# Two-block chunks at the start, earlier W1, and engine orders written out, in a fused windowed-attention and feed-forward kernel

## The chip, the cores and the metric

The kernel runs on one core of a Trainium2 chip. A core has a matrix engine (TensorE, PE in the profile, with its weight loads shown as PEld), a vector engine (VectorE, DVE), an activation engine (ScalarE, ACT), a general engine (GpSimd, POOL) and SyncE (SP), which here only issues transfers. They run side by side, each through its own instructions in order, and wait for each other by semaphores. Transfers that POOL issues go through a software queue, and they change f32 to f16 on the way; those that SP issues go through a hardware queue.

The metric is the time of one execution on the device, in microseconds (us). The kernel before takes 310.35 us, the median of three runs (307.21 to 311.88).

## The reference

Inputs are q, k and v with 8 batches, 8 heads, 576 positions and a head size of 64, a gain vector of 512, and two weight matrices W1 (512 x 2048) and W2 (2048 x 512). All are f32.

```python
scores = (q @ k.T) / sqrt(64)
bias   = slope[h] * -abs(i - j)              # slope[h] = 2 ** -(h + 1)
mask   = (i - j >= 0) & (i - j < 128)
scores = where(mask, scores + bias, -1e9)
attn   = exp(scores - max(scores)); attn = attn / (sum(attn) + 1e-9)
x      = (attn @ v), heads side by side      # 8 x 576 x 512
xn     = (x - mean(x)) / sqrt(var(x) + 1e-6) * g
out    = x + maximum(xn @ W1, 0) @ W2
```

## The kernel before

**Blocks and chunks.** The 8 x 576 rows make 36 blocks of 128 rows. A row sees 128 keys back, so a block needs its own keys and those of the block before it; the first block of a pair of batches needs only its own. The list BLOCK puts the first two blocks of three of these pairs in front (places 0 to 5), then the rest. Blocks gather in chunks for the feed-forward part: CHUNKS has three chunks of 3, 3 and 2 blocks and seven of 4.

**Attention of block i** (function `attention`, L638). q and k are loaded, turned so that the head dimension lies on partitions (T tasks on TensorE with an evacuation ev or eT, or from block 9 on a transposing DMA, QT), and multiplied: S (L811). For the first five blocks a bias product Z (L827) puts distance and causality into the scores before S; from block 5 on the exp is multiplied by a table: mka and mkb (L866), one for each half of the heads. exa and exb are the exp on ACT (L859). pva and pvb (L887) multiply with v, which has a column of ones, so that the sum of a row comes with it; rc (L904) and nm (L908) divide. bn and ag take the statistics, mu and xs normalise (L947 for early chunks, L971 later), and x is turned by TX (L985) with an evacuation xt, or from block 6 on by a transposing DMA, XT.

**Loads.** Blocks 0 to 5 (SPANS = 0, 2, 4) come in pairs: `load_span` (L555) loads two blocks of q or k in f32 through SP, half of the heads at a time or all; casts cT (L706) on DVE, ACT or POOL make f16; T (L726) turns two f16 at a time as one f32. From block 6 (LOAD_CAST) q and k come through POOL's software queue as f16 (L573). v comes so from block 1 on. The weights, four parts of W1 (w0 to w3, L628) and four of W2 (w4 to w7, L630), come through the same queue.

**Feed-forward of chunk c** (function `mlp`, L1268). Chunks below SEVEN = 3 are plain: a task A{c}.{f} (L1285) multiplies one of 16 groups of W1's columns with the chunk's x, over four matmuls of up to 384 columns, into one PSUM bank; r{c}.{f} (L1300 on ACT, L1298 on DVE) is the relu; B{i}.{f} (L1319) multiplies with W2 and o adds x. Later chunks use seven products in place of eight, with sums made on DVE, for W2 (Pa to Pg, L1071), and from chunk BOTH = 8 on for W1 too (Ua to Ug, L1200). scaleW multiplies the gain into W1 before chunk SEVEN; earlier chunks multiply it into x.

**What sets the order.** Every step is a task with the engines that could do it, its costs and what it depends on. `Plan.run` (L131) plays the tasks through with a heap: on each engine it starts the ready task with the lowest due time, corrected by the tables PRI and HOLD; PICK says which engines a task may use, QUEUE in which order POOL's transfers go. What comes out is the order in which each engine's instructions are written. FILL (L274) puts products of a constant tile (`keep_warm`, L1366, matmuls at L1368) before named TensorE tasks; their result is never read. Masks may run on DVE or POOL by `e_m` (L863 to L866); PICK leaves them to the default, DVE.

```python
en = nc.vector if e == "DVE" else nc.gpsimd
en.tensor_tensor(out=pv, in0=pv, in1=mask[:, 2 * half : 2 * half + 2, :, lo:], op=ALU.mult)
```

Of the kernel before, what the change touches and what calls it, by code (L numbers as in the profile page):

```python
# [16 lines left out]
class Task:  # L17
    __slots__ = ("eng", "emit", "deps", "v", "lat", "acq", "rel", "left", "users", "ready", "end", "start", "name", "room", "chain")

    def __init__(self, name, eng, emit, deps, v, lat, acq, rel):  # L20
        self.name, self.eng, self.emit, self.v, self.lat = name, eng, emit, v, lat
        self.deps = [d for d in deps if d is not None]
        self.acq, self.rel = ([acq] if isinstance(acq, tuple) else acq or []), rel
        self.users, self.ready, self.end, self.start, self.room = [], 0.0, None, None, 0.0
        self.chain = []
# [29 lines left out]

class Plan:

    OVERLAP = {"ACT": 0.10, "DVE": 0.07, "POOL": 0.05}
    QUEUE_ROOM = {'DMA SP': 4.0, 'DMA ACT': 4.0, 'DMA POOL': 8.0}
    BEGIN = 0.75
    LANDING = {"DMA SP": (0.7, 1.3), "DMA ACT": (0.7, 1.3), "DMA POOL": (2.1, 1.4)}
    SHARES = {
        (True, 512): (0.66, 0.32), (True, 256): (0.66, 0.32), (True, 2048): (0.7, 0.4),
        (False, 512): (0.5, 0.5), (False, 256): (0.5, 0.5), (False, 2048): (0.5, 0.5),
    }
    LAST_OF_RUN = 1.0  # L70
    BEHIND = (2.5, 1.5)
    PRI: dict = {}
    HOLD: dict = {}
# [9 lines left out]
    def add(self, name, eng, emit, deps=(), v=0.0, lat=None, acq=None, rel=None):  # L83
        if not isinstance(eng, dict):
            eng = dict([eng])
        if lat is None:
            lat = 0.2 if "PE" in eng else 0.05 + max(self.OVERLAP.get(e, 0.0) for e in eng)
        eng = {e: c - self.OVERLAP.get(e, 0.0) for e, c in eng.items()}
        t = Task(name, eng, emit, deps, v + self.PRI.get(name, 0.0), lat, acq, rel)
        t.ready = self.HOLD.get(name, 0.0)  # L90
        self.tasks.append(t)
        return t

    def transfer(self, name, eng, issue, secs, room, emit, deps=(), v=0.0):

        queue = "DMA " + eng
        i = self.add(name + ".i", (eng, issue), emit, deps, v, lat=self.LANDING[queue][0])
        d = self.add(name, (queue, secs), None, [i], v, lat=self.LANDING[queue][1])
        i.room = d.room = room
        return i, d  # L100

    SLACK: tuple = (0, 0.4, 0)

    def slack(self, t, when):

        if "DMA POOL" in t.eng:
            return self.SLACK[2]
        return self.SLACK[0] if when < 30.0 else self.SLACK[1]

    def rates(self, queues):  # L110
        on = [q for q, x in queues.items() if x]
        if "DMA POOL" in on and len(on) > 1:
            others = [queues[q][0][0].name for q in on if q != "DMA POOL"]
            size = 512 if any(n[:2] in ("qs", "ks") for n in others) else 256 if any(n[0] in "qkv" for n in others) else 2048
            weight = queues["DMA POOL"][0][0].name[0] == "w"
            a, b = self.SHARES[weight, size]
            return {q: a if q == "DMA POOL" else b / (len(on) - 1) for q in on}
        return {q: 1.0 / len(on) for q in on}

    def skew(self, queue, now):  # L120

        if now >= 60.0:
            return 0.0
        early = 1.6 if self.early else 0.0
        if queue == "DMA POOL":
            return min(1.1, max(0.0, (now - 11.5) * 0.4)) + early
        if queue == "DMA SP" and now < 24.0:
            return (0.6 if self.mixed else 0.15) + early
        return 0.0

    def run(self):  # L131
        self.mixed = self.early = False
        again = []
        for r in self.rings:
            r.link()
        for t in self.tasks:
            t.left = len(t.deps) + len(t.chain)
            for d in t.deps + t.chain:
                d.users.append(t)
        engines = sorted({e for t in self.tasks for e in t.eng if not e.startswith("DMA")})  # L140
        queues = {e: [] for e in sorted({e for t in self.tasks for e in t.eng if e.startswith("DMA")})}
        free = dict.fromkeys(engines, self.BEGIN)
        avail = {e: [] for e in engines}
        state = {p: {b: self.opens.get((p, b), 0.0) for b in bs} for p, bs in self.banks.items()}
        held, waits, used = {}, {}, dict.fromkeys(queues, 0.0)
        for t in self.tasks:
            if t.rel is not None:
                waits[t.rel] = waits.get(t.rel, 0) + 1
        heap, n = [], 0
        for t in self.tasks:  # L150
            if t.left == 0:
                heap.append((max(self.BEGIN, t.ready), n, t))
                n += 1
        for x in self.opens.values():
            heap.append((x, n, None))
            n += 1
        heapq.heapify(heap)
        self.order, left, now = [], len(self.tasks), 0.0

        def done(t):  # L160
            nonlocal n
            for u in t.users:
                late = self.slack(t, t.end) if "PE" in u.eng and "PE" not in t.eng else 0.0
                u.ready = max(u.ready, t.end + (0.0 if t in u.chain else t.lat + late))
                u.left -= 1
                if u.left == 0:
                    heapq.heappush(heap, (u.ready, n, u))
                    n += 1

        def bank(t):  # L170
            got = []
            for p, key in t.acq:
                if key in held:
                    continue
                open_ = [(when, b) for b, when in state[p].items() if when is not None and when <= now + 1e-9]
                if not open_:
                    return False, None
                got.append((p, key, min(open_)[1]))
            return True, got

        while left:
            while heap and heap[0][0] <= now + 1e-9:
                t = heapq.heappop(heap)[2]
                if t is None:
                    continue
                for e in t.eng:
                    if e in queues:
                        if e == "DMA SP" and not queues[e] and queues["DMA POOL"] and t not in again:
                            again.append(t)
                            heapq.heappush(heap, (now + self.BEHIND[now >= 24.0], n, t))  # L190
                            n += 1
# [92 lines left out]
def kernel(  # L284
# [15 lines left out]
    P = 128  # L300
# [1109 lines left out]
```

## Time and profile before

| | |
|---|---|
| three timed runs | 307.21, 310.35, 311.88 us |
| span of the profiled execution, first to last instruction | 305.0 us |
| time around the span | not on the page; the timed runs are 2.2 to 6.8 us longer than the span |
| granted TensorE clock, mean | 1.000 |
| busy in 0 to 7 us: PE, DVE, ACT, POOL | 5.51 (60 filler matmuls), 2.01, 1.28, 1.38 of 7 |
| busy in 26.74 to 60 us: PE, DVE, ACT, POOL | 33.26, 28.64, 20.79, 22.54 of 33.26 |
| busy in 110 to 200 us: PE, DVE, ACT, POOL | 89.86, 75.19, 50.79, 38.38 of 90 |
| busy in 200 to 305 us: PE, DVE, ACT, POOL | 101.69, 87.19, 47.41, 0.00 of 105 |

The page's first part gives busy time of each engine over the span; the timeline lists instructions in order of time, neighbours of one kind merged, with the start, the time taken, the engine, the source line, and what is written and read (out<-in, buffer numbers left out); behind them in brackets the idle time before and what ended it. The waits view sums who waited for whom. TensorE's matmuls overlap, so a group's busy time is longer than the distance between starts times their number.

### The profile page before, as it was taken

To read this page: it belongs to the slowest core of one execution; us is meant where nothing else is said; L and a number is where in the kernel's file an instruction comes from. 1 tells how busy PE (TensorE), PEld (TensorE's weight loads), DVE (VectorE), ACT (ScalarE), POOL (GpSimd) and SP (SyncE) were. 2 spreads that over 40 slices of the span, in tenths; PEclk is the share of its full clock that TensorE was granted. 3 is DMA by queue.
4 is the path that set the end of the run, shared out by engine and by line. 5 is a ranking of instruction groups with operands and counts; after the bars stand their busy time and mean duration, and the time that the engine had idled before them with its cause. 6 is when DMAs were issued, how large, how long until landed. Compare 5 with 4: busy or idle time off the path is not lost.

```text
span 305.0 us, 7454 instructions
## 1 busy us (share of the span) xinstructions
PE 297.5 (98%) x2984; PEld 220.5 (72%) x2984; DVE 244.7 (80%) x597; ACT 164.8 (54%) x281; POOL 101.4 (33%) x132
## 2 busy tenths in 40 slices
PE   7989999999999999999999999999999999999995
PEld 7777756665774558765877577856777799999984
DVE  2778998677997479947983988999987889897883
ACT  1467943746776696436442956487733755235400
POOL 2993558735654337545405633100000000000000
PEclk9999999999999999999999999999999999999999
DMA  7999999999999999999999999961301500030043
GB/s 202 269 192 202 203 168 164 164 132 144 189 174 156 172 160 148 140 147 186 195 146 138 225 155 171 136 189 37 37 5 31 169 6 0 2 139 2 29 145 105
DMA packets 159652, 40.99 MB, mean 134 GB/s; under 512 B 145793, under 2 KB 155009, under 8 KB 159618
## 3 DMA queue, kind: packets, MB, share of 16 engines
q0 software_dynamic: 101680, 16.65, 76.9%
q1 hardware_dynamic: 57936, 23.87, 43.8%
q8 instruction: 23, 0.38, 0.5%
q14 instruction: 11, 0.09, 0.1%
q10 hardware_dynamic: 2, 0.00, 0.0%
HBM read 36.70 MB, written 9.44 MB: 151 GB/s over the span
## 4 chain that ended last, share of the span: by engine, by line
PE 86%; DMA 4%; DVE 4%; ACT 3%; issue 1%; SPq 0%; POOL 0%
PE fb L1285 30%; PE fb L1071 27%; PE u L1200 8%; PE fb L1319 7%; PE sc L811 5%; PE fb L887 5%; DMA qkt<-qk 3%; DMA qs<-in_q_dram 1%; ACT probs L859 1%; ACT ht L1300 1%; PE fb L726 1%; DVE st L927 1%; PE fb L1368 1%; DVE xb L908 1%; PE sc L827 1%
## 5 line engine op out<-in xcount | busy, mean ns | idle before, releaser
L1285 PE MATMUL fb<-xt,w1sb 128*128 128x512 f16 (+2 forms) x512 | 108.2, 353 | 0.6 <-DVE ot L1327 0.2
L859 ACT ACTIVATE probs<-sc 128x1024 f16<-128x1024 f32 (+1 forms) x72 | 67.9, 975 | 32.4 <-PE sc L811 30.9
L1300 ACT ACTIVATE ht<-fb 128x512 f16<-128x512 f32 (+2 forms) x109 | 58.3, 548 | 43.3 <-PE fb L1285 39.5
L1285 PEld LDWEIGHTS <-w1sb 128*128 128x128 f16 x512 | 55.2, 114 | 33.1 <-issue 1.3
L1071 PEld LDWEIGHTS <-ht 128*128 128x128 f16 x560 | 53.1, 98 | 9.9
L1071 PE MATMUL fb<-w2sb,ht 128*128 128x256 f16 x336 | 44.9, 273 | 0.0
L573 POOL DMA_DIRECT2D qk<-in_k_dram x34 | 28.7, 845 | 33.3 <-DMA qkt<-qk 23.5
L573 POOL DMA_DIRECT2D vx<-in_v_dram x36 | 30.7, 865 | 20.8 <-PE fb L887 8.2
L573 POOL DMA_DIRECT2D qk<-in_q_dram x34 | 28.8, 854 | 26.3 <-DMA qkt<-qk 12.8
L1071 PE MATMUL fb<-ks,ht 128*128 128x256 f16 x224 | 31.4, 273 | 0.0
L1319 PE MATMUL fb<-w2sb,ht 128*128 128x512 f16 x128 | 30.8, 379 | 0.2 <-ACT ht L1300 0.2
L866 DVE TENSOR_TENSOR probs<-probs,mreg 128x1024 f16<-128x1024 f16 (+1 forms) x46 | 30.1, 664 | 0.5 <-ACT probs L859 0.4
L887 PEld LDWEIGHTS <-probs 128*128 128x128 f16 x544 | 24.7, 97 | 7.5 <-ACT probs L859 0.6
L908 DVE SCALAR_TENSOR_TENSOR xb<-fb,rec 128x256 f16<-128x256 f32 x72 | 29.4, 416 | 0.8
L887 PE MATMUL fb<-vx,probs 128*128 128x65 f16 x496 | 27.2, 193 | 0.8 <-DVE xb L908 0.6
L904 DVE RECIPROCAL rec<-fb 128x4 f32<-128x4 f32 x72 | 12.2, 173 | 18.2 <-PE fb L887 18.0
L1083 DVE TENSOR_TENSOR ot<-fb,xb 128x512 f32<-128x512 f32 (+1 forms) x31 | 19.5, 634 | 7.2 <-PE fb L1071 6.7
L927 DVE BATCH_NORM_STATS2 st<-xb 128x6 f32<-128x512 f16 x36 | 24.4, 682 | 0.1
L811 PEld LDWEIGHTS <-qkt 64*128 64x128 f16 x496 | 14.9, 94 | 8.3 <-issue 7.4
L1223 DVE TENSOR_TENSOR ht<-u,probs 128x512 f16<-128x512 f32 x24 | 16.1, 686 | 5.3 <-PE u L1200 3.9
L1319 PEld LDWEIGHTS <-ht 128*128 128x128 f16 x128 | 11.4, 97 | 11.7 <-ACT ht L1300 0.4
L1213 ACT ACTIVATE probs<-u 128x512 f32<-128x512 f32 x21 | 12.2, 597 | 12.3 <-PE u L1200 12.2
(117 smaller groups left out, 397.0 us busy)
## 6 DMA issues: line engine op xcount, KB each, us to landing
out_dram<-ot SPq DMA_DIRECT2D x32, 256.0 KB, 3.6
vx<-in_v_dram POOLq DMA_DIRECT2D x28, 128.0 KB, 11.0
qk<-in_q_dram POOLq DMA_DIRECT2D x26, 128.0 KB, 11.2
qk<-in_k_dram POOLq DMA_DIRECT2D x26, 128.0 KB, 11.5
w1sb<-in_moe_w_ch_dram POOLq DMA_DIRECT2D x4, 512.0 KB, 10.6
w2sb<-in_moe_w_ch_dram POOLq DMA_DIRECT2D x4, 512.0 KB, 14.0
ks<-in_k_dram SPq DMA_DIRECT2D x4, 256.0 KB, 4.0
qs<-in_q_dram SPq DMA_DIRECT2D x4, 256.0 KB, 5.0
```

Source lines behind the costliest of these rows:

```text
L573: nc.gpsimd.dma_start(out=dst(p0, n), in_=src[b, :, s0 : s0 + n, :].rearrange("h p d -> p h d"))
L811: nc.tensor.matmul(scs[half][:, g, c0 : c0 + P], kt[rows, 1, hp, :], qkt[i][rows, 0, hp, :], start=not bias, stop=True, skip_group_check=True,
L859: nc.scalar.activation(out=o, in_=n_, func=AF.Exp, scale=inv_sqrt_d)
L866: en.tensor_tensor(out=pv, in0=pv, in1=mask[:, 2 * half : 2 * half + 2, :, lo:], op=ALU.mult)
L887: nc.tensor.matmul(pp[:, hh * (D + 1) : hh * (D + 1) + D + 1], probs[i][:, bank, slot, side * P : side * P + P], vx[i if side else before] ...
L908: nc.vector.scalar_tensor_tensor(out=xb[c][:, j, 256 * half : 256 * half + 256].rearrange("p (h d) -> p h d", d=D), in0=pp[:, :, 0:D], sca ...
L927: nc.vector.bn_stats(out=st[i][:, :], in_=xb[c][:, j, :])
L1071: nc.tensor.matmul(o, lhs(f, p), rhs(f), start=first and f == 0 and (p == 0 or key[0] != key[1]), stop=f == F2 - 1, skip_group_check=True)
L1200: nc.tensor.matmul(late[bank][:, FOURTH * f : FOURTH * f + FOURTH], w, rhs[kb], start=first and f == kb == 0, stop=kb == 1, skip_group_che ...
L1285: nc.tensor.matmul(fb[b][:, 0:n_], w1f[f // CB][:, kb, f % CB, :], xt[c][:, kb, 0:n_], start=(kb == 0), stop=(kb == NKB - 1),)
L1300: nc.scalar.activation(out=ht[c][:, f, 0:n_], in_=src, func=AF.Relu)
L1319: nc.tensor.matmul(pm[:, 0 : c1 - c0], ht[c][:, f, j * P : j * P + P], w2sb[f // CB][:, f % CB, c0:c1], start=(f == 0), stop=(f == NFB - 1),)
```

## The change

- CHUNKS begins with four chunks of two blocks in place of 3, 3 and 2. SEVEN and BOTH move by one, so that the same blocks are plain, and the same use seven products.
- In a two-block chunk, a task A{c}.{f} makes two groups of W1's columns, 256 columns each, into one bank, and one relu reads both. There are 8 such tasks for a chunk.
- Only blocks 0 and 1 are loaded as a span; q and k of blocks 2 to 5 come through POOL's queue as f16 and are turned one block at a time (T2 to T5). Only blocks 0 and 1 have their scores in two halves (SPLIT).
- The planner goes. ORDER is a text that names every task in the order of writing, with its engine (A for ACT, V for DVE, T for TensorE, G for POOL, S for SP) and, for TensorE, its PSUM bank; ~n stands for n filler matmuls. `Plan.run` reads it and asserts that what a task depends on stands before it. PRI, HOLD, PICK, QUEUE and FILL go. The engines of tasks are those that ORDER names: of the 62 masks, 44 stand on G and 18 on V. The fillers sum to 76, all before the 22nd TensorE task.
- On POOL, w0 stands behind the cast of the first half of k; w3, w1 and w2 follow behind q, k and v of blocks 2 and 3.

```diff
-QUEUE = ['cT0.00', 'cv0', 'v1', 'cT2.01', 'dist', 'dist1', 'v5', 'cT0.11', 'v2', 'dist1b', 'v3', 'w0', 'w3', 'w2', 'v4', 'w6', 'w1', 'dist1a', 'q6', 'k6', 'w4', 'w5', 'w7']
-FILL = {'T0.0': 60, 'G': 1, 'Gk': 1, 'Zb1': 9, 'T0.1': 4, 'Sb1': 13, 'Sa0': 1, 'pvb1': 10, 'pva0': 2, 'pvb0': 8, 'pva2': 10, 'Sa3': 1, 'pva3': 6}
...
+def Choice(names, full):
+    return dict(full)
...
     def run(self):
+
+        by, done, order, users = {}, set(), [], {}
+            by.setdefault(t.name, []).append(t)
+                users[t.rel] = users.get(t.rel, 0) + 1
+        owner, self.held = {}, {}
+
+        def ready(t):
+            if t.emit is None and id(t) not in done:
+                if all(ready(d) for d in t.deps):
+                    done.add(id(t))
+            return id(t) in done
+
+        for word in ORDER.split():
+            if word[0] == "~":
+                order.append((None, int(word[1:]), None))
+                continue
+            name, where = word.split(":")
+            t, e, b = by[name].pop(0), self.ENGINES[where[0]], int(where[1:]) if where[1:] else None
+            assert e in t.eng and all(ready(d) for d in t.deps), name
+            for n, (p, key) in enumerate(t.acq):
+                if key not in self.held:
+                    bank = b if n == 0 else self.banks[p][0]
+                    assert bank in self.banks[p] and owner.get((p, bank)) is None, name
+                    owner[p, bank], self.held[key] = key, (p, bank)
+            if t.rel is not None:
+                users[t.rel] -= 1
+                if users[t.rel] == 0:
+                    owner[self.held[t.rel]] = None
+            done.add(id(t))
+            order.append((t, e, self.held[t.acq[0][1]][1] if t.acq else None))
+        assert all(t.emit is None for ts in by.values() for t in ts)
+        return order
+
+
+ORDER = """
+iden1:G qs0.0.i:S iden2:G ks0.0.i:S dist:G sid0:V iden3:V dist00:G qs1.0.i:S sid6:V dist01:G sid5:V ks1.0.i:S sid3:V sid2:V sid7:V sid1:V sid4:V
+v0.i:S ~38 Za0:T0 cT0.00:A g.i:A cT0.10:G w0.i:G ~19 T0.0:T0 cT0.01:G eT0.00:V cT0.11:V q2.i:G ~7 Sa0:T0 eT0.01:V Zb0:T0 exa0:A T0.1:T1 k2.i:G Za1:T0
+eT0.10:V cv0:A v1.i:G eT0.11:A Sa1:T0 Sb0:T0 G:T2 q3.i:G exb0:A exa1:A k3.i:G Zb1:T0 Gc:V w3.i:G Sb1:T0 pvb0:T0 pva0:T1 exb1:A Gk:T2 v2.i:G rc1.0:V
+rc0.0:V nm0.0:V nm1.0:V v3.i:G ~8 T2:T1 mu0:V xs0:V Z2:T0 w1.i:G pva1:T0 ev2:V pvb1:T3 w2.i:G rc0.1:V Gkc:V S2:T0 rc1.1:V nm0.1:V k4.i:G TX0:T1
+nm1.1:V exa2:A T3:T2 bn0:V w4.i:G exb2:A mu1:V ev3:A xs1:V ~4 Z3:T0 w5.i:G bn1:V w6.i:G TX1:T0 S3:T0 xt1:A xt0:V q4.i:G exa3:A A0.14:T3 w7.i:G exb3:A
+A0.0:T2 r0.14:V pva3:T1 r0.0:A pva2:T0 A0.2:T3 rc0.3:V nm0.3:V rc0.2:V k6.i:G pvb3:T2 r0.2:V A0.12:T1 rc1.3:V nm0.2:V pvb2:T3 Z4:T0 nm1.3:V A0.6:T0
+rc1.2:V mu3:V xs3:V k5.i:G A0.4:T2 r0.6:A nm1.2:V r0.12:A mu2:V q5.i:G TX3:T3 xs2:V A0.8:T0 xt3:A ag0:V bn3:V TX2:T1 r0.8:A A0.10:T3 xt2:V r0.4:A
+ag3:V ag1:V bn2:V A1.6:T0 v4.i:G r0.10:V A1.4:T1 r1.6:A A1.12:T2 r1.4:A ln0:A A1.0:T3 q6.i:G rs0:A r1.12:A B0.0:T0 r1.0:V B1.0:T1 k7.i:G A1.2:T2
+B1.4:T1 q8.i:G B0.4:T0 T4:T3 B1.8:T1 ev4:V q7.i:G r1.2:V B0.8:T0 k8.i:G B1.12:T1 k8.i:G B0.12:T0 o1.0:V k9.i:G S4:T0 ag2:V sumT1.0:V A1.14:T3 q8.i:G
+exa4:A o0.0:V exb4:A T5:T2 q9.i:G sumT1.1:V r1.14:A A1.8:T1 ev5:V k10.i:G pva4:T0 pvb4:T3 S5:T0 mreg30:A rc1.4:V v5.i:G nm1.4:V mreg10:A T6:T2 exa5:A
+rc0.4:V nm0.4:V B3.0:T3 q11.i:G ev6:V mreg20:A B2.0:T0 mreg00:A r1.8:V q10.i:G exb5:A mu4:V A1.10:T2 xs4:V k11.i:G mreg01:A mreg11:A sumT0.0:V B3.4:T3
...
+"""
...
-    CHUNKS = [3, 3, 2, 4, 4, 4, 4, 4, 4, 4]
+    CHUNKS = [2, 2, 2, 2, 4, 4, 4, 4, 4, 4, 4]
-    WARM = 24.0
+    WARM = 14.0
-    SPLIT = 4
-    LOAD_CAST = 6
+    SPLIT = 2
+    LOAD_CAST = 2
-    BY_HALVES = [0, 2, 5]
+    BY_HALVES = [0]
-    SPANS = [0, 2, 4]
-    SLACK = (0, 1.0, 0)
-    SEVEN = 3
-    BOTH = 8
+    SPANS = [0]
+    SEVEN = 4
+    BOTH = 9
...
-            return {e: cost[e] for e in PICK.get((name, i), default).split()}
+            return Choice(default, cost)
...
+        two = 2 if nb == 2 else 1
         for at, f in enumerate(order):
+            if f % two:
+                continue
             key = f"A{c}.{f}"
             vm = v0 + at * per
 
             def e_a(e, b, f=f):
-                for kb in range(NKB):
-                    nc.tensor.matmul(
-                        fb[b][:, 0:n_], w1f[f // CB][:, kb, f % CB, :], xt[c][:, kb, 0:n_],
-                        start=(kb == 0), stop=(kb == NKB - 1),
-                    )
-            a = add(key, ("PE", 0.216 * nb), e_a, done + [scaled[f // CB] if fast else t_w[f // CB][1]], vm, acq=("fb", key))
+                for x in range(two):
+                    for kb in range(NKB):
+                        nc.tensor.matmul(
+                            fb[b][:, n_ * x : n_ * x + n_], w1f[f // CB][:, kb, (f + x) % CB, :], xt[c][:, kb, 0:n_],
+                            start=(kb == x == 0), stop=(kb == NKB - 1), skip_group_check=two > 1,
+                        )
+            a = add(key, ("PE", 0.216 * nb * two), e_a, done + [scaled[f // CB] if fast else t_w[f // CB][1]], vm, acq=("fb", key))
             xt.reads(c, a)
             plain_all[f // CB].append(a)
             if not fast:
                 plain[f // CB].append(a)
 
             def e_r(e, b, f=f, key=key):
-                src = fb[plan.held[key][1]][:, 0:n_]
+                src, o = fb[plan.held[key][1]][:, 0 : n_ * two], ht[c][:, f, 0:n_]
+                if two > 1:
+                    src, o = src.rearrange("p (f c) -> p f c", f=two), ht[c][:, f : f + two, 0:n_]
                 if e == "DVE":
-                    nc.vector.tensor_scalar(out=ht[c][:, f, 0:n_], in0=src, scalar1=0.0, scalar2=None, op0=ALU.max)
+                    nc.vector.tensor_scalar(out=o, in0=src, scalar1=0.0, scalar2=None, op0=ALU.max)
                 else:
-                    nc.scalar.activation(out=ht[c][:, f, 0:n_], in_=src, func=AF.Relu)
-            r_ = add(f"r{c}.{f}", {"ACT": 0.17 + 0.107 * nb, "DVE": 0.16 + 0.133 * nb}, e_r, [a], vm - 4.0, rel=key)
+                    nc.scalar.activation(out=o, in_=src, func=AF.Relu)
+            r_ = add(f"r{c}.{f}", Choice("ACT DVE", {"ACT": 0.17 + 0.107 * nb * two, "DVE": 0.16 + 0.133 * nb * two}), e_r, [a], vm - 4.0, rel=key)
             ht.writes(c, r_)
-            relu[f] = r_
+            for x in range(two):
+                relu[f + x] = r_
...
         for t, e, b in order:
-            if e == "PE":
-                keep_warm(FILL.get(t.name, 0))
+            if t is None:
+                keep_warm(e)
+                continue
```

More of the change, by code (lines that the diff above doesn't have):

```diff
@@ L1 @@
-import heapq
 from contextlib import ExitStack
@@ L94, in transfer @@
     def transfer(self, name, eng, issue, secs, room, emit, deps=(), v=0.0):
[L96 to L99, printed above, removed]
+        i = self.add(name + ".i", (eng, issue), emit, deps, v)
+        d = self.add(name, ("DMA " + eng, secs), None, [i], v)
         return i, d
[L102 to L118, printed above, removed]
@@ L160, in done @@
[L160 to L179, printed above, removed]
```

254 lines of the change are left out of this document (89 added, 165 removed).

## The prediction

> **What bounds the kernel now.** First the page: which engine is full, and where it is not.
>
> ```profile
> span 305.0 us, 7454 instructions
> PE 297.5 (98%) x2984; PEld 220.5 (72%) x2984; DVE 244.7 (80%) x597; ACT 164.8 (54%) x281; POOL 101.4 (33%) x132
> PE 86%; DMA 4%; DVE 4%; ACT 3%; issue 1%; SPq 0%; POOL 0%
> ```
>
> TensorE is busy 98% of the span and makes 86% of the chain that ended last. A busy PE may still do nothing useful, so next the timeline of PE, to the first feed-forward product.
>
> ```profile
> 1.06 5.51 PE L1368 MATMUL fb<-warm_t 128*128 128x128 f16 x60 [1.06 <-DVE warm_t L462]
> 7.12 0.44 PE L726 MATMUL fb<-iden,qs 128*128 128x128 f32 x2 [0.55 <-POOL qs L706]
> ...
> 25.66 0.39 PE L985 MATMUL fb<-iden,xs 128*128 128x128 f16 x4
> ...
> 26.74 3.50 PE L1285 MATMUL fb<-xt,w1sb 128*128 128x384 f16 x20
> ```
>
> L1368 is filler that computes nothing. The line groups give 126 fillers, 11.2 us, all before 26.74. Product A of chunk 0 starts at 26.74, after the third block's turn (L985) at 25.66. Counting what PE had done by then, at the start-to-start times in the trace: 24 f32 turns by 0.110 us (2.6), gain products 2.0, bias products 16 by 0.109 and 24 by 0.055 (3.1), 56 score products by 0.037 (2.1), 48 PV products by 0.035 (1.7), 12 turns of x by 0.06 (0.7): 12.2 us of use in 26.7.
>
> Behind 26.74 I listed the gaps between matmul starts more than 0.1 us over the usual step: 7 of them, 2.5 us together, of 278.3 us. The waits view of PE for that time agrees.
>
> ```profile
> PE sc L811 <- DMA qkt<-qk: 0.6, 1, 0.6
> PE fb L1319 <- ACT ht L1300: 0.2, 1, 0.2
> ```
>
> So there are two prices: what comes before 26.74 can shrink by microseconds, what comes after by 2.5 at most, unless the amount of work changes.
>
> **The amount of work on PE** hardly does. Plain A products: before, 128 of 384 columns (step 0.162) and 64 of 256 (0.109), 27.7 us; after, 4 chunks by 64 of 256, 256 by 0.109, 27.9. Turns of q and k: before 24 f32 by 0.110 and 24 f16 by 0.056, 4.0; after 8 and 56, 4.0. Plain B and the later chunks are the same (BOTH and SEVEN still cover the same blocks). Fillers fall from 126 to 76, but stand in waits. Sum: +0.2.
>
> **The start, step by step.** Landings are the semaphore marks in the trace.
> - HWDGE loads. Before, ten 256 KB or 512 KB loads stand on SP; the first three land at 3.76, 4.58, 6.26, and q's first half is only third. After, five, in the order q, k, q, k, v. By the same places q lands at 3.8 and k at 4.6. The half casts: POOL 0.75 (6.31 here), ACT 0.79. T0.0 goes from 7.12 to about 5.5. This alone is worth little, since 26.74 hangs on later things.
> - Software queue. Before, its first issue is at 8.02 (v1, landing 14.37), the first packets at 11.9, 2.9 us after that issue ended. W tiles then come every 2.5 us (w0 at 21.42, w3 24.43, w2 26.48, w1 32.34), a q, k or v block every 0.87. After, w0 is issued behind the cast of k's half: 5.4 to 6.15, packets from about 9.0, data through at 11.5, landing 1.4 later (the last v here: data through at 17.6, landing 18.97): 12.9. The written order then gives q2 13.8, k2 14.6, v1 15.5, q3 16.4, k3 17.2, w3 19.7, v2 20.6, v3 21.4, w1 23.9, w2 26.4, w4 29.8, w5 32.3, w6 34.8, w7 38.2. Four q and k blocks move from HWDGE to this queue: 8 by 0.87, 7 us of queue time, counted in these dates. SP has nothing else until the transposes.
> - Chain of block 1, which ends in xt1: v1 15.5, pva1 15.6, then in DVE's written order reciprocals 0.17, normalisations 0.42, bn 0.66, mean 0.21, xs 0.75: xs1 done at 18.8; TX1 0.3, xt1 on ACT 0.59 behind ev3 (k3 17.2, T3 0.5, ev3 1.02, so 18.9): 19.7.
> - So the first A product, A0.14 (W1 part 3), is ready at about 19.8 by both paths, xt1 19.7 and w3 19.7, against 26.74: **-6.9**. With packets 2.1 us behind the issue, not 2.9, it is 19.0.
> - What is then not yet done that was done before: T4 and T5 (16 by 0.056), Z4 0.44, S4 0.3, PV of blocks 2 and 3 (24 by 0.035), TX2 0.25: **+2.7**.
> - Does W keep up? Pairs take 8 by 0.109, 0.87 us. A0.6 (w1) is reached at 24.5 against 23.9, A0.8 (w2) 26.5 against 26.4, B0.0 (w4) 32.0 against 29.8, B1.8 (w6) 36.8 against 34.8, B1.12 (w7) 38.5 against 38.2. Margins of 0.1 to 2.3 us: each late microsecond is soon one on the end. I put **+0.5** here.
>
> **Off the path.** Paired relus: 36 of 384 or 256 columns become 21 on ACT (0.597) and 11 on DVE (0.684): ACT -3.6 us, DVE +1.1, beside PE. Two span casts and their halves leave DVE and POOL, about 4 us. DVE is full from 35 to 50 (14.73 of 15 us) while PE is too (15.00), so PE's cover there is the queue of A and B products.
>
> **Masks move to POOL**, which the change's name doesn't say. The page before has no mask on POOL: 62 stand on DVE (L866), mean 0.675. The written order sends 44 to POOL, 18 to DVE: DVE -29.7 us. No row shows a two-input product on POOL; nearest is the CAST of 1024 elements, 1.35. POOL: 101.4 + 44 by 1.35 = 161 us, and its DMA issues (0.86) queue behind a mask that waits for ACT's exp. Loads run some 11 us ahead of their landing, which covers this. But one row speaks against it:
>
> ```profile
> 18.54 2.09 DVE L947 SCALAR_TENSOR_TENSOR xs<-xb,mean,g_t 128x512 f16<-128x512 f16 x1
> 22.77 0.75 DVE L947 SCALAR_TENSOR_TENSOR xs<-xb,mean,g_t 128x512 f16<-128x512 f16 x1
> ...
> 18.77 1.35 POOL L706 CAST qs<-ht 128x1024 f16<-128x1024 f32 x1
> ```
>
> The same xs takes 0.75 alone and 2.09 beside POOL's cast: 1.34 more, the cast's own length. So a mask on POOL saves DVE 0.675 or costs it up to 0.67. Of 44, from 0 to 44 meet such an operation: DVE between -29.7 and +29.3. About one shared operation starts each 2.3 us in these stages, so some 20 meet: about -10 us, off the path. On PE: nothing, ends -2.5 (its gaps go) and +8 (below). The Trainium skill's page "SBUF — State Buffer", section "SBUF: two separate sides", says the port pair of DVE and GpSimd is an exclusive lock held for a whole instruction; the trace agrees (1.34 of 1.35). Its page "GPSIMD Engine Reference", section "Elementwise — side-by-side cycle accounting", gives 2.6 cycles an element for two inputs; at its 1.2 GHz I estimate 2.2 us a mask, and POOL at 198 us. No run here shows that yet.
>
> **Sum:** +0.2 - 6.9 + 2.7 + 0.5 = -3.5 us, a span of 301.5. The page gives no time around the span; the three timed runs are 2.2 to 6.8 longer than it, the median 5.3. I keep 5.3: **306.8 us** against 310.35, 1.1% less. A measurement of this kernel can tell about 2% from no change, 6.2 us.
>
> **Rivals.**
> - *The later stages gain too* (chance 0.22). The new order also removes the 2.5 us of gaps, DVE being lighter, and A0.14 starts at 19.0: -7.7 + 2.7 + 0.2 - 2.5 = -7.3, 303.0. For: the gaps at 81 to 109 are waits for DVE, ACT and one transposing DMA. Against: most are 0.1 to 0.4 us each.
> - *W arrives late* (0.15). Before, one W tile took 3.0 us, not 2.5, and POOL waited 3.0 us for landings before two W2 issues. At 3.0 a tile the seventh behind w0 is 3.5 us late and only 0.3 is spare: 306.8 + 3.2 = 310.0. The gain is lost between 20 and 40 us.
> - *Masks on POOL collide* (0.15, slower). Place: blocks 5 to 35, from 40 to 225 us. At 35 to 50 DVE has 0.27 us spare in 15; from 150 to 250 14.3 in 100. If all meet, 8 early masks cost 8 by 0.67 = 5.4 us there, and each of the 44 arrives 1.34 us late at its PV product, behind which PE waits in order; if a fifth exceed their cover, 9 by 0.7 = 6. Together 306.8 + 5.4 + 6 - 2 for the slack of queued products: 316. It decides from about one meeting in two, or from 2 us a mask.
> - The rest, 0.48, is the forecast.
>
> **Range.** The forecast reaches 304 to 309 by the 0.8 us of queue start and the spread of the three runs (-3.1, +1.5). Over the rivals at both sides: 301.5 to 313. Faster by over 2% (under 304.1): most of the first rival and a little of the forecast, 0.25. Slower (over 316.6): half of the third, 0.08. Within: 0.67.
>
> **What would show it.** A first A product at 19 to 20.5 us, with the seven W tiles landing as dated: the start is right; at 23 or later, W or the software queue was late. PE gaps over 0.1 us behind it: about 3 us in all; 8 or more, with PV products waiting for POOL's masks, is the third rival. POOL masks of 1.4 us, DVE near 235 us busy. It would be wrong if the software queue shares with SP's loads longer than I allow, or if PE, with fewer fillers in the start's waits, ran its first A products at longer steps than 0.109.

## The result, and the profile after

The changed kernel takes **345.99 us** (median of four runs, 345.85 to 346.57), the kernel before, beside it, 310.33 (307.21 to 311.88). The ratio is **1.120, 95% interval 1.114 to 1.125**: slower by 12%. Ratios here and below compare fast executions alone (none over 1.5% above the fastest of its kernel), so they need not be the ratios of the medians. Forecast was 306.8, range 301.5 to 313.0. The profiled execution took 346.11 us, its span is 344.4.

First the page of the kernel after, its first parts and the head of its chain:

```profile
span 344.4 us, 7504 instructions
...
PE 308.4 (90%) x3014; PEld 228.5 (66%) x3014; DVE 280.5 (81%) x555; ACT 155.2 (45%) x256; POOL 200.4 (58%) x183
...
PEclk9999998996999988999999899998998999999999
...
PE 23%; DVE 3%; issue 0%; DVEq 0%
```

TensorE falls from 98% to 90% busy. VectorE was to lose 29.7 us of masks and has 35.8 more than before (244.7). The granted clock, 1.000 before, has holes (0.960 in the mean); what they cost is worked out below. The chain followed from the end reaches back over a quarter of the span only, so it says little here.

Where does the time go? The timeline of PE shows that the start is as forecast: the first A product is the last line.

```profile
1.06 4.22 PE L1287 MATMUL fb<-warm_t 128*128 128x128 f16 x38 [1.06 <-DVE warm_t L387]
...
18.12 0.40 PE L906 MATMUL fb<-iden,xs 128*128 128x128 f16 x4 [0.24 <-DVE xs L868]
...
19.21 1.91 PE L1210 MATMUL fb<-xt,w1sb 128*128 128x256 f16 x16
```

It starts at 19.21 instead of 26.74. So the loss lies behind it. The waits view of PE (us in total, times, longest) names VectorE, not the masks on GpSimd:

```profile
PE fb L992 <- DVE ot L1004: 8.9, 6, 2.4
PE fb L1210 <- DVE xb L829: 7.2, 3, 3.4
PE fb L808 <- DVE ht L1225: 4.5, 1, 4.5
PE fb L906 <- DVE xb L829: 3.0, 1, 3.0
PE fb L808 <- POOL probs L787: 1.9, 2, 1.0
```

The groups of the page say what became of VectorE (busy us, mean ns of one, then idle before it):

```profile
L787 POOL TENSOR_TENSOR probs<-probs,mreg 128x1024 f16<-128x1024 f16 (+1 forms) x34 | 72.7, 2145 | 39.9 <-ACT probs L780 39.9
L892 DVE TENSOR_SCALAR xs<-xb,mv,rstd 128x512 f16<-128x512 f16 x28 | 26.3, 955 | 1.4 <-ACT rstd L885 1.3
```

A mask on GpSimd takes 2.14 us, against 0.675 on VectorE before. And the xs that stays on VectorE takes 0.955 us in place of 0.413, with nothing changed in it. One place shows how. The timelines of DVE, POOL and PE, 50 to 59 us:

```profile
50.32 5.58 DVE L466 COPY mmix<-mreg 128x2048 f16<-128x2048 f16 x1
55.82 0.23 DVE L825 RECIPROCAL rec<-fb 128x4 f32<-128x4 f32 x2
...
57.13 1.75 DVE L868 SCALAR_TENSOR_TENSOR xs<-xb,mean,g_t 128x512 f16<-128x512 f16 x1
```

```profile
49.37 2.19 POOL L787 TENSOR_TENSOR probs<-probs,mreg 128x1024 f16<-128x1024 f16 x1
51.44 0.94 POOL L496 DMA_DIRECT2D vx<-in_v_dram  x1
52.40 2.13 POOL L787 TENSOR_TENSOR probs<-probs,mreg 128x1024 f16<-128x1024 f16 x1
54.46 0.95 POOL L496 DMA_DIRECT2D qk<-in_k_dram  x1
```

```profile
52.52 1.04 PE L1247 MATMUL fb<-w2sb,ht 128*128 128x512 f16 x4
56.51 0.59 PE L906 MATMUL fb<-iden,xs 128*128 128x128 f16 x4 [2.95 <-DVE xb L829]
```

The copy at 50.32 took 0.685 us before. Here it takes 5.58: it lasts over a mask, a transfer issue, a second mask and a second issue. The reciprocal and the normalisation queued behind it are 4.9 us late, TensorE runs out of work at about 53.5 and stands 2.95 us.

**The whole difference in one sum.** I list the steps from one matmul's start to the next that are over 0.1 us longer than the usual step of their shape, behind 26.7 us, and call the excess a stall. Span = start of the first A product + these stalls + a rest, and the rest is nearly the same in kernels of one structure, up to 3 us more where the granted clock fell:

| kernel | span | first A | stalls (number) | rest |
|---|---|---|---|---|
| before | 305.0 | 26.74 | 2.6 (8) | 275.7 |
| after | 344.4 | 19.21 | 45.8 (88) | 279.4 |
| e1_masks_dve | 306.1 | 19.91 | 7.7 (19) | 278.5 |
| e2b_before_pool_masks | 356.0 | 27.15 | 50.7 (98) | 278.2 |
| e3_idle_products | 389.5 | 20.53 | 88.1 (165) | 280.9 |
| e4c_one_fill | 302.2 | 20.23 | 3.7 (6) | 278.3 |
| e4b_two_fills | 307.8 | 19.38 | 9.8 (18) | 278.6 |
| e4d_two_and_quarter | 325.4 | 21.16 | 24.7 (51) | 279.5 |
| e4_write_only | 347.4 | 21.16 | 45.8 (67) | 280.4 |
| e10_quarter_masks | 313.6 | 20.86 | 14.5 (22) | 278.2 |
| e9_half_masks | 319.5 | 19.11 | 21.8 (38) | 278.6 |
| e5_hybrid | 307.3 | 20.27 | 8.9 (15) | 278.1 |
| e6_relu_act | 306.0 | 19.14 | 8.1 (18) | 278.8 |
| e7_before_relu_act | 307.9 | 27.39 | 5.0 (12) | 275.5 |
| e8_nine_moves | 305.2 | 20.40 | 6.6 (23) | 278.2 |

After against before: -7.5 at the start, +43.2 of stalls, +3.7 of rest: +39.4.

**The stalls are of two kinds.** I counted them a second time, with the usual steps of the kernel before and of e1, and apart: waits, in which TensorE is idle, and slower steps, in which one matmul follows the other without idle time. The kernel after has 26 waits of 34.5 us together, and slower steps of 11.7 us in seven stretches, 27.3 us together, in which the granted clock is 0.50. (Outside such stretches, steps without idle time are about 2 us over the usual in e1 as in the kernel after. The sum is 46.2, not 45.8, since excesses under 0.1 us count in the stretches.) One place, in PE's timeline and in the windows view, which gives the stretch, the busy us and number of instructions of PE, PEld, DVE, ACT and POOL, the granted clock, the DMA share and GB/s:

```profile
121.27 3.94 PE L1210 MATMUL fb<-xt,w1sb 128*128 128x512 f16 x10 [2.52 <-DVE xb L829]
```

```profile
121.20:124.60 3.40, 3.33 (x8) 1.18 (x8) 2.68 (x9) 0.00 (x0) 0.00 (x0) 0.50 0.39 113
```

TensorE waits 2.52 us for VectorE's xb; the eight products in the stretch then take 3.33 us, 0.42 each, where the usual step of this shape is 0.216. Each of the seven stretches begins between 1.7 us before and 0.9 us after the end of a wait of 1.5 to 4.7 us. Not every such wait is followed by one: a wait of 3.0 us in e10 is not. Behind 26.7 us, its last microseconds aside, neither the kernel before nor e1 has such a stretch.

### The profile page after: what moved, and what is told of

The parts are those of the page before. It is cut to its first block, busy times and chain, and to the rows that moved or that the text cites. A ratio compares the mean times of both kernels' runs of the same rounds, so it can differ in the third digit from the quotient of the medians.

```text
span 344.4 us, 7504 instructions
## 1 busy us (share of the span) xinstructions
PE 308.4 (90%) x3014; PEld 228.5 (66%) x3014; DVE 280.5 (81%) x555; ACT 155.2 (45%) x256; POOL 200.4 (58%) x183
## 5 line engine op out<-in xcount | busy, mean ns | idle before, releaser
L1210 PE MATMUL fb<-xt,w1sb 128*128 128x512 f16 (+1 forms) x576 | 113.1, 343 | 10.5 <-DVE xb L829 7.2
L787 POOL TENSOR_TENSOR probs<-probs,mreg 128x1024 f16<-128x1024 f16 (+1 forms) x34 | 72.7, 2145 | 39.9 <-ACT probs L780 39.9
L1210 PEld LDWEIGHTS <-w1sb 128*128 128x128 f16 x576 | 63.2, 115 | 42.3 <-issue 19.0
L1227 ACT ACTIVATE ht<-fb 128x512 f16<-128x512 f32 x78 | 45.4, 595 | 59.8 <-PE fb L1210 49.3
L992 PEld LDWEIGHTS <-ht 128*128 128x128 f16 x560 | 53.8, 98 | 15.0 <-issue 5.5
L496 POOL DMA_DIRECT2D qk<-in_k_dram x38 | 33.1, 872 | 11.6 <-DMA qkt<-qk 5.0
L496 POOL DMA_DIRECT2D qk<-in_q_dram x38 | 33.2, 875 | 3.8 <-DMA w2sb<-in_moe_w_ch_dram 3.4
L808 PEld LDWEIGHTS <-probs 128*128 128x128 f16 x544 | 24.0, 98 | 15.9 <-issue 7.4
L1225 DVE TENSOR_SCALAR ht<-fb 128x512 f16<-128x512 f32 x34 | 23.0, 682 | 13.8 <-PE fb L1210 13.8
L1247 PE MATMUL fb<-w2sb,ht 128*128 128x512 f16 x128 | 33.7, 403 | 0.1
L892 DVE TENSOR_SCALAR xs<-xb,mv,rstd 128x512 f16<-128x512 f16 x28 | 26.3, 955 | 1.4 <-ACT rstd L885 1.3
L1004 DVE TENSOR_TENSOR ot<-fb,xb 128x512 f32<-128x512 f32 (+1 forms) x31 | 19.6, 634 | 8.0 <-PE fb L992 7.8
L732 PEld LDWEIGHTS <-qkt 64*128 64x128 f16 x496 | 15.9, 99 | 7.6 <-issue 6.2
L1247 PEld LDWEIGHTS <-ht 128*128 128x128 f16 x128 | 12.1, 102 | 12.4 <-issue 2.6
```

The source lines that it names most:

```text
L496: nc.gpsimd.dma_start(out=dst(p0, n), in_=src[b, :, s0 : s0 + n, :].rearrange("h p d -> p h d"))
L808: nc.tensor.matmul(pp[:, hh * (D + 1) : hh * (D + 1) + D + 1], probs[i][:, bank, slot, side * P : side * P + P], vx[i if side else before] ...
L892: nc.vector.tensor_scalar(out=xs[x][:, :], in0=xb[c][:, y, :], scalar1=mv[c][:, y, 0:1], scalar2=rstd[c][:, y : y + 1], op0=ALU.subtract, ...
L992: nc.tensor.matmul(o, lhs(f, p), rhs(f), start=first and f == 0 and (p == 0 or key[0] != key[1]), stop=f == F2 - 1, skip_group_check=True)
L1210: nc.tensor.matmul(fb[b][:, n_ * x : n_ * x + n_], w1f[f // CB][:, kb, (f + x) % CB, :], xt[c][:, kb, 0:n_], start=(kb == x == 0), stop=(k ...
L1227: nc.scalar.activation(out=o, in_=src, func=AF.Relu)
```

## The experiments

Theories: (1) the 44 masks on GpSimd are the loss, and the rest of the change is worth a little; within that, (a) each mask holds VectorE while it runs, (b) the mask comes later to its PV product, or GpSimd's queue is full. Rival (2): the order written out, or the two-block chunks, are the loss.

e2, e2b, e3, the four of e4, e9 and e10 were run once each. Ten executions of e1 have spans of 306.1 (the profiled one) to 308.9, so a difference of 2 or 3 us between single runs says little.

**e1_masks_dve: the masks alone taken back.** 44 words of the order change; nothing else.

```diff
-... exb6:A mkb5:G T8:T2 ...
+... exb6:A mkb5:V T8:T2 ...
```

> The changed kernel with its 44 GpSimd masks back on VectorE, at the same places of the order; nothing else differs. Theory (masks on GpSimd hold up VectorE, and through it TensorE): the gaps behind 50 us go, span 299 to 304 us, VectorE near 245 us busy, the mmix copy 0.7 us. Rival (the written order or the two-block chunks are what costs): still above 330 us. Rival (masks cost, but the order needs VectorE's freed 30 us): 310 to 325 us, VectorE full.

Measured: 308.69 us against 309.64 before, ratio 1.001 (0.998 to 1.004), span 306.1. The page's busy times, and from the groups of DVE the masks, the xs and the copy:

```profile
PE 295.5 (97%) x3014; PEld 224.4 (73%) x3014; DVE 251.9 (82%) x599; ACT 155.1 (51%) x256; POOL 106.2 (35%) x139
```

```profile
L787 DVE TENSOR_TENSOR probs<-probs,mreg 128x1024 f16<-128x1024 f16 x44 | 29.8, 679 | 0.7 <-ACT probs L780 0.6
...
L892 DVE TENSOR_SCALAR xs<-xb,mv,rstd 128x512 f16<-128x512 f16 x28 | 12.1, 445 | 1.8 <-ACT rstd L885 0.9 <-DMA xt<-xs 0.8
...
L466 DVE COPY mmix<-mreg 128x2048 f16<-128x2048 f16 x1 | 0.7, 749 | 0.0
```

With 44 masks more in its queue, about 29 us of work, VectorE is 28.6 us *less* busy than in the kernel after. xs is back to 0.445, the copy to 0.749. The masks are the loss, all 38.3 us of it: stalls 45.8 to 7.7 are 38.1. By the second count, waits fall from 34.5 to 6.8 and slower steps from 11.7 to nothing: the granted clock is back at 1.000. I had expected a span of 299 to 304, or, by the third theory, 310 to 325; it lies between. What is left of the change, with the masks where they were, is worth nothing: -6.8 at the start, +5.1 of stalls, +2.8 of rest.

**e2 and e2b: the masks alone put into the kernel before.** The first edit (e2) put entries for GpSimd ahead of entries of the same names in the table PICK, which then won: its trace has all 62 masks on VectorE, and its time, 307.84 us, is one more of the kernel before. It decides nothing.

> The kernel before with the same 44 masks given to GpSimd; its planner orders the rest around them. Theory (masks on GpSimd cost by themselves): slower by 20 us or more, masks of 2.1 us, VectorE operations of several microseconds, granted clock under 1. Rival (the loss needs the new order): within 8 us of before.

e2b moves the same 44 behind the planner, at their places in its order:

```diff
     order = plan.run()
+    order = [(t, "POOL" if t is not None and t.name in moved else e, b) for t, e, b in order]
```

> The kernel before with its order as planned, and only the same 44 masks issued on GpSimd in place of VectorE. Theory (masks on GpSimd cost the time by themselves: 2.14 us of latency each in place of 0.69, and VectorE held beside them): span 340 to 380, since this order leaves even less time between exp and PV. Rival (the loss belongs to the rest of the change, the order written out or the chunks): span within 5 us of 305.

Measured: 357.75 us, span 356.0. So the masks cost 51 us in the old order, where nothing else of the change is made: more than in the new one (38). Rival (2) falls. The groups show VectorE held in the same way, in its own masks too, 1.606 us against 0.68 where they run alone; but here TensorE waits for GpSimd's masks as well, 8.3 us against 1.9 in the kernel after, so (b) has a part in this order:

```profile
L971 DVE TENSOR_SCALAR xs<-xb,mv,rstd 128x512 f16<-128x512 f16 x28 | 30.8, 1118 | 2.3 <-ACT rstd L964 2.2
...
L866 DVE TENSOR_TENSOR probs<-probs,mreg 128x1024 f16<-128x1024 f16 x12 | 19.3, 1606 | 0.5 <-ACT probs L859 0.5
```

```profile
PE fb L887 <- POOL probs L866: 8.3, 5, 3.5
```

**e3_idle_products: holding alone.** e1, and at the place of each moved mask a product on GpSimd of two constant tables into a scratch tile that nobody reads.

```diff
                 en.tensor_tensor(out=pv, in0=pv, in1=mask[:, 2 * half : 2 * half + 2, :, lo:], op=ALU.mult)
+                if f"mk{'ab'[half]}{i}" in MOVED:
+                    nc.gpsimd.tensor_tensor(out=idle_t[:, :, :, lo:], in0=mask[:, 0:2, :, lo:], in1=mask[:, 2:4, :, lo:], op=ALU.mult)
```

> All masks on VectorE as in the run without GpSimd masks, and 44 products of the constant mask tables into a scratch tile on GpSimd where the masks stood; nobody waits for them. The output is the reference's. Theory (GpSimd's reading holds VectorE's operations): VectorE operations stretch as in the changed kernel, 330 to 350 us. Rival (what costs is that the PV products wait for slow masks): close to the run without GpSimd masks, under 310 us.

Measured: 391.19 us, span 389.5, some 40 us above the theory's range, and TensorE never waits for GpSimd. The groups of DVE show which of its instructions are held, and which are not (line numbers are two to four higher here):

```profile
L789 DVE TENSOR_TENSOR probs<-probs,mreg 128x1024 f16<-128x1024 f16 (+1 forms) x46 | 62.3, 1357 | 0.5 <-ACT probs L782 0.4
L833 DVE SCALAR_TENSOR_TENSOR xb<-fb,rec 128x256 f16<-128x256 f32 x72 | 29.3, 416 | 1.0
L852 DVE BATCH_NORM_STATS2 st<-xb 128x6 f32<-128x512 f16 x36 | 24.1, 679 | 0.1
...
L986 DVE TENSOR_TENSOR ht<-ht,ks 128x1024 f16<-128x1024 f16 x14 | 18.6, 1329 | 0.0
```

Masks (1.357 us against 0.668 for the same group of e1) and W2's sums (1.329 against 0.678) are held; the normalisations that read PSUM (0.416) and the statistics (0.679) keep their times (0.417 and 0.681 in e1), but stand behind the held ones. Holding, with no delay of a PV product by GpSimd, can thus lose 83 us when VectorE has all its masks as well: against e1, 60.9 more of waits and 22.4 of slower steps. VectorE has 44 masks more here than in the kernel after, which are held too and have to be done besides.

**e4: delay, with less holding.** The kernel after, each GpSimd mask replaced by fills of the same tile, which read nothing: three, two and a quarter, two, and one.

```diff
-                en.tensor_tensor(out=pv, in0=pv, in1=mask[...], op=ALU.mult)
+                for _ in range(3):
+                    nc.gpsimd.memset(pv, 1.0)
```

> The changed kernel with each of the 44 GpSimd masks replaced by three GpSimd fills of the same tile with ones: the exp's weights are lost there, so the output is not the reference's. GpSimd is still between exp and PV product, but reads nothing. Theory (the shared reading is what holds VectorE's two-input operations): the two-input sums and masks on VectorE return to 0.68 us; the one-input xs (0.41 us before) may still be held. 300 to 320 us. Rival (slow GpSimd work between exp and PV): 335 us or more if the three fills take 2 us together.

> The kernel after with each GpSimd mask replaced by two fills of 1.0 (about 1.9 us, near the 2.14 us of the mask), which read nothing; the weights of the exp are lost. Three fills gave a span of 347.4. Theory (the delay between exp and PV has a threshold near what the order was written for): 310 to 325. Rival (what costs goes with the time that GpSimd is busy): 306 + 41 x 2/3 = 333. If the delay explained the whole loss of the kernel after, a mask of 1.9 us should stand near 335 to 344.

> The same with one fill (about 0.95 us) in place of each GpSimd mask; the weights of the exp are lost. Theory of the delay with a threshold: the order has time for it, VectorE is 30 us lighter than with its own masks, span 299 to 304. Rival (cost goes with GpSimd's busy time): 306 + 41 / 3 = 320.

> The kernel after with each GpSimd mask replaced by two fills and a fill of a quarter, about 2.2 us in place of the mask's 2.14, reading nothing; the weights of the exp are lost. Two fills (1.9 us) gave a span of 307.8, three (2.84 us) 347.4, the masks themselves 344.4. If the held VectorE makes most of the loss, this stays at 310 to 322. If the delay between exp and PV makes most of it, with a threshold between 1.9 and 2.14 us, it stands at 335 to 345.

A fill takes 0.97 us, one of a quarter 0.33. Spans: one fill 302.2, two (1.94 us) 307.8, two and a quarter (2.27) 325.4, three (2.9) 347.4. One and three are as expected, three by the rival's 335 or more; two stands below its theory's 310 to 325. Groups and PE's waits of the run with two and a quarter:

```profile
L896 DVE TENSOR_SCALAR xs<-xb,mv,rstd 128x512 f16<-128x512 f16 x28 | 21.2, 770 | 1.5 <-ACT rstd L889 1.5
...
L986 DVE TENSOR_TENSOR qs<-ht 128x1024 f16<-128x1024 f16 x14 | 9.6, 682 | 0.2
```

```profile
PE fb L812 <- POOL probs L791: 15.9, 7, 4.3
```

In all four, VectorE has 44 masks less than in e1 (233.1 us busy with one fill, 251.9 in e1). Three things follow. VectorE's sums of two inputs are free again (0.682); xs is still held, but less (0.770). Now the PV products do wait for GpSimd. And the price is no slope but an edge: from one fill to two it rises by 5.6 us, for the next third of a microsecond by 17.6 (waits +11.1, slower steps +4.4, and a start that came 1.8 later). Why there: between its first mask, at about 50 us, and its last, GpSimd's queue also has 86 transfer issues of 0.87 us, 75 us. With one fill it is busy 120 us of the 173 of that stretch, with two 159 of 182, with two and a quarter 172 of 198, with three 200 of 220. It takes its queue in order and waits for ACT's exp at the head (17 to 20 us in the last three). With two fills it is busy 87% of the stretch and as good as full: 13.6 us of work more lengthen the stretch by 16. With the masks themselves it is busy 171.5 us of 216, 79%. My expectation for two and a quarter had "310 to 322" for holding and "335 to 345" for delay: 325.4 is between, so this run doesn't divide the loss.

**e9 and e10: half and a quarter of the masks left on GpSimd.** Its queue is then not full (125 of 181 us, 101 of 165), but each mask left holds VectorE as before.

```diff
-... mkb5:G ... mkb6:G ... mka6:G ... mkb7:G ...
+... mkb5:G ... mkb6:V ... mka6:G ... mkb7:V ...
```

> The kernel after with every second of its 44 GpSimd masks moved back to VectorE, 22 left on GpSimd. From the first mask at 49 us on GpSimd has 75 us of transfer issues; with 44 masks of 2.14 us that made 171 us of work for a stretch that takes 173 us when fills of 0.95 us stand there; with 22 it makes 122. Theory A (the loss is GpSimd's queue being full): it goes almost wholly, span 303 to 311. Theory B (the loss is VectorE held by each mask that meets it): it halves, 306 + 19 = 325, from 318 to 332.

> The same with every fourth mask left on GpSimd, 11 of 44. Theory A: 302 to 306, since VectorE is 7 us lighter and GpSimd far from full. Theory B: 306 + 38 / 4 = 315, from 311 to 320.

Measured: span 319.5 and 313.6 (321.19 and 315.31 us). PE's waits with half the masks are for VectorE again, hardly for GpSimd:

```profile
PE fb L992 <- DVE ot L1004: 8.1, 5, 3.7
...
PE fb L808 <- POOL probs L787: 1.5, 2, 1.0
```

With 0, 11, 22 and 44 masks on GpSimd the span is 306.1, 313.6, 319.5 and 344.4: about 0.6 us for each of the first 22, 1.13 for each of the others. Theory A would have had 303 to 311 and 302 to 306, and falls; both runs lie in B's ranges. What the steeper second half is made of, by the second count (us); holding is VectorE's busy time less that of e1 without the masks that moved, 0.668 us each:

| kernel | masks on GpSimd | span | waits (number) | slower steps | holding |
|---|---|---|---|---|---|
| e1_masks_dve | 0 | 306.1 | 6.8 (16) | 0 | 0 |
| e10_quarter_masks | 11 | 313.6 | 13.7 (21) | 0 | 12.1 |
| e9_half_masks | 22 | 319.5 | 18.9 (21) | 2.5 | 23.7 |
| after | 44 | 344.4 | 34.5 (26) | 11.7 | 58.0 |

The waits grow by about 0.6 us a mask from end to end: 0.55 for each of the first 22, 0.71 for each of the others, with more holding a mask (1.08, then 1.56 us). They make 27.7 of the 38.3 us. Most of the bend is the slower steps: 11.7 us, of which the first 22 masks have 2.5. (The start came 0.7 earlier than in e1.) A full queue of GpSimd shows no part of its own: TensorE's waits for GpSimd's masks are 1.9 us in the kernel after, where they are 15.9 with two and a quarter fills. Why holding rises with the number of masks, and why some waits bring the lower clock and others don't, stays open.

**e6, e7, e5, e8: is the start's gain to be had with the masks on VectorE?** e1 has 7.7 us of stalls where the kernel before has 2.6. Four ways to get them back were tried. e6 puts the order's 34 relus of VectorE on ScalarE (VectorE is then 231.9 us busy, not 251.9), e7 does the same in the kernel before, e5 keeps the new order to the last plain product and takes the old planner's order behind it, and e8 moves instructions at nine stalls, such as:

```diff
-... mka17:V Pa4.11:T3 xs14:V pvb16:T1 sb4.1:V S18:T0 XT14.i:S ra4.0:V ...
+... mka17:V Pa4.11:T3 xs14:V pvb16:T1 ra4.0:V sb4.1:V S18:T0 XT14.i:S ...
```

> The kernel after with all masks on VectorE, and the 34 relus that its order has on VectorE (682 ns each, 23 us in all) on ScalarE (596 ns each there) at the same places. With the masks back the span was 306.1, with some 8.3 us of stalls behind the first A product. Theory (this order needs a VectorE some 30 us lighter, however it is made so): stalls fall to 2 to 5 us, span 300 to 303.5, ratio 0.975 to 0.99. Rival (the stalls come from when the masks stand in VectorE's queue, not from how full it is): span 305 to 307, ratio within 0.995 to 1.005.

> The kernel before, its order as planned, with the relus that the plan has on VectorE issued on ScalarE at the same places. Theory (the stalls are an affair of the order written out; the kernel before has only 2.5 us of them to lose): span 303 to 306, ratio 0.99 to 1.005. Rival (every order here gains from a lighter VectorE, so that a gain of the run beside it is none of this change's): ratio under 0.99.

> The start of the kernel after (its order up to the last plain product, about 100 us), all masks on VectorE, and behind it the order of the kernel before, with its chunks renumbered. Theory (the start's gain is real, and the stalls behind 50 us come from an order that was written for masks on GpSimd): the stalls over 0.1 us behind the first A product, 8.3 us with masks moved back, fall to some 4, and the span from 306.1 to 300 to 303, the time to 302 to 306, a ratio of 0.97 to 0.99 to the kernel before. Rival (two-block chunks leave later stages that cannot run as tightly, whatever the order): the stalls stay at 7 to 9 us and the span at 305 to 307.

> The kernel after with all masks on VectorE, and nine places of VectorE's order changed: at nine of the stalls behind 50 us, the instruction that frees a bank (or, at one, the mask that a PV waits for) goes ahead of a mask, a sum or a statistic that nobody waits for yet. Theory (the 8 us of stalls come from where the masks stand in VectorE's queue): the stalls at these places lose 0.3 to 1.2 us each, 3.5 to 5 us together, span 301.5 to 303.5, ratio 0.983 to 0.994. Rival (each repair brings the next wait): span 305 to 306.5, ratio within 0.995 to 1.005.

| run | ratio to before | interval | stalls |
|---|---|---|---|
| e6_relu_act | 1.003 | 0.999 to 1.007 | 8.1 |
| e7_before_relu_act | 1.004 | 1.000 to 1.008 | 5.0 |
| e5_hybrid | 1.002 | 0.999 to 1.006 | 8.9 |
| e8_nine_moves | 0.998 | 0.996 to 1.001 | 6.6 |

None beats the kernel before. In e6 the two largest stalls stay, at 116.3 (1.24 us in e1, now 1.76) and 221.1 (1.32, now 1.31), each before a product that waits for a bank whose reader (L1004) stands behind masks and xs: at these two it is the place in the queue, not how full VectorE is, and e6's theory falls. e5 loses 3.1 us at 95 to 97 where the two orders are joined. e8 loses 1.1 us of stalls, not the 3.5 to 5 expected: it shrinks those it aimed at (116.8: 1.24 to 0.43, 221: 1.32 to 0.39), and new ones appear at 66, 81, 82 and 220.9. Only e4c, whose GpSimd masks compute nothing, has the gain, in its one run: 303.88 us, where the fastest execution of the kernel before took 306.08. Why the gain can't be had with the masks, beyond "each repair brings the next wait", stays open.

## Why the prediction was wrong, step by step

- **The start: right.** A first A product "at about 19.8" came at 19.21, and at 19.1 to 21.2 in the runs with the same start. The landings stand in the order given and 0.5 to 1.7 us before their dates (w0 11.19, v1 15.03, k3 16.01, w3 18.58, w1 22.84, w2 25.41, w4 28.69, w5 31.20, w6 33.85, w7 37.01). The cautious guess of 2.9 us from issue to packets was too long (w0's issue ends at 6.25, the queue's first packet starts at 7.01), the rival's 19.0 the better date.
- **What is left behind and the work on PE: right as a sum.** +2.7 and +0.2 forecast; the rest of e1 is 2.8 above that of the kernel before.
- **W late: no.** The margins held: PE has no stall over 0.1 us between 19.3 and 50 us.
- **Masks move to POOL, "on PE: nothing": the step that failed.** The sum put this term at nothing. It left out a wait: held by GpSimd's masks, VectorE is late with what frees TensorE's banks. Against e1, TensorE waits 27.7 us more, and the slower steps that come with the waits make 11.7; the whole is 38 us. I called the holding "off the path" with VectorE 80% full. The sizes inside it were off too. A mask was put at 1.35 us by the CAST, and took 2.14; the estimate of 2.2 from the Trainium skill's page "GPSIMD Engine Reference", section "Elementwise — side-by-side cycle accounting", set beside it, was the right one, and POOL's 200.4 us are its 198. Of the 44 masks I let 20 meet an instruction that they hold; in the trace 33 run beside one that lasts over 0.2 us longer than its kind in e1. With its 18 masks left VectorE should have had 251.9 less about 29 by e1, 223, and had 280.5: 58 us of holding, 1.3 us for each of the 44. As a total that is the upper end that I had written down (VectorE +29.3; measured +28.6 against e1, +35.8 against the kernel before); that 1.3 is near the 1.34 of the row that I showed is chance, since it is a mean over masks of 2.14 us, of which a quarter held nothing. And my middle was added up wrong: 20 meetings of 1.34 less 29.7 make -2.9 us, not "about -10", so VectorE near 242, not 235.
- **The third rival: right in cause and place, wrong in the wait, 30 us too low.** Its mark was "8 or more, with PV products waiting for POOL's masks". The gaps were 45.8, but the waits are for VectorE's xb, ot and ht; the PV products that wait for GpSimd make 1.9 us. I let each held instruction cost once, at 5.4 + 6; but a held copy keeps back everything queued behind it, and nothing in the sum stood for a lower clock. It was to decide "from about one meeting in two, or from 2 us a mask": 33 of 44 and 2.14 us pass both, and I gave it 0.15.
- **A second error that the first one hides.** Even with the masks back the change is worth nothing: I had the later stages at 2.5 us of stalls or fewer, and with e1's order they have 7.7; why is open (e6 to e8).
- **Around the span** I kept 5.3 us, the distance of the median of the timed runs from one profiled span. Each profiled execution lies 1.7 to 2.2 above its own span, the kernel before 2.2 (the 2.2 to 6.8 of the table of before compares other executions with one span); the rest of the 5.3 was the spread of executions.

On the lock: the Trainium skill's page "SBUF — State Buffer", section "SBUF: two separate sides", names as the instructions of VectorE that take it those in a two-port performance mode, and those with two SBUF inputs, the latter only against a GpSimd operation that reads SBUF. The runs agree: against products the sums took 1.329 us, against fills 0.68, while xs, with one tile as input, was held by both (0.955 and, with one fill to three, 0.567 to 0.788; alone 0.41 to 0.45). That xs runs in a two-port mode no run shows. Where I had used only its "whole instruction", this clause said which of VectorE's work was exposed.

## What to carry to other kernels

Before moving work from VectorE to GpSimd, list which VectorE instructions beside it go from f16 tiles in SBUF to f16 tiles in SBUF (masks, sums, xs and copies here; not the statistics, nor what reads PSUM). Each may last as long as the GpSimd instruction or longer, and what is queued behind it is late as well, so VectorE can end busier than it was (280.5 against 251.9 us here). Add up the other engine's queue over the stretch where the moved work must be done, its transfer issues too, and not over the span: with two fills GpSimd is 61% busy on the page and 87% in that stretch, and there work added to it lengthened the stretch by more than itself. When TensorE has waited, look at the granted clock behind the wait: 11.7 us of the loss were matmuls at 0.50 of it. And read the diff, not the title: 44 words of an order cost more than all the rest of the change moved.

## What the runs showed that was not expected

- One f16 copy on VectorE (0.685 us alone) lasted 5.58 us, over two masks of GpSimd and two transfer issues between and behind them. It was not done in the 0.84 us between the two masks, in which it would have had the time.
- Fills that read nothing still hold xs (0.77 us with two and a quarter, against 0.41 to 0.45).
- Of the loss, 11.7 us are steps in seven stretches of granted clock 0.50, which begin around the end of TensorE's waits.
- GpSimd's price for TensorE has an edge: 44 times 1.94 us cost 5.6 us more than 44 times 0.97, and 44 times 2.27 another 17.6.
- In several runs of the new start the granted clock is lower between 10 and 20 us (0.79 in 10 to 15 us and 0.87 in 15 to 20 in e8_nine_moves, 1.00 in e1_masks_dve), with first A products at 20.4 and 19.9.
